# Attention and maxout feed-forward on one core: the start of batch 0 put in another order

## The chip, the cores and the metric

The kernel runs on one core of one Trainium2 chip. The metric is the device time of one execution in microseconds (us); the time given for a kernel is the median of its runs. A profiled execution also has a span, which runs from the first to the last recorded instruction and is a little shorter than the device time of that same execution.

## The reference

Two layers stand one behind the other. The first is attention with a softmax whose denominator has one more term; the second is a feed-forward layer that takes the maximum of three products.

```python
scores = scale * np.matmul(q, k.transpose(0, 1, 3, 2))
m = np.max(scores, axis=-1, keepdims=True)
e = np.exp(scores - m)
attn = e / (np.sum(e, axis=-1, keepdims=True) + np.exp(-m) + 1e-09)
return np.matmul(attn, v)
...
h = np.maximum(np.maximum(x @ w1, x @ w2), x @ w3)
return h @ w_out
```

q, k and v have 8 batches, 12 heads, 448 positions and 64 columns, in float32. x is the attention output with its heads side by side: 3584 rows of 768. The four weights are 768 x 768.

## The kernel before

**Tiling.** A batch's 12 heads are three groups of four heads, and a group is two pairs of heads. Groups are numbered through: 0, 1 and 2 are batch 0, group 3 is the first of batch 1, and there are 24. For one group the kernel loads k, q and v (POOL issues these DMAs, which turn float32 into float16 on the way), turns q and k over on TensorE (`transpose_pe`, L183, in two halves `pr` 0 and 1; `transpose_once`, L213, a whole q or k), and copies the result from PSUM to the tiles `KT` and `QT` (`evac`, L177, on ScalarE, "ACT", or VectorE, "DVE"). `scores` (L281) multiplies K by Q and takes the exponential on ACT into one of two buffers `e`. `av` (L523, by `av_tail` and `av_main`) multiplies the exponentials by V and then divides by the sum on DVE, for one pair of heads. `x_transpose_pe` (L387) turns the result over into `xT`, the input of the feed-forward. `prep_v` (L376) lays v out for `av` in three copies, `vx` and twice `vt`.

**Parts of batch 0.** While the data still come in, groups 0 to 2 are done in two parts of the query positions: the part "O" (192 columns) of each group and then the part "E" (256 columns). From group 3 on both parts go together ("EO").

**Feed-forward.** Its work lies in a list of pieces, and `fill` (L506) takes the next ones from it wherever the written order has a place for them. An `up_piece` (L430) is 12 matmuls of line 435 for one weight matrix and two blocks of columns, and its result goes into `hT` by a copy (first matrix) or a maximum (second and third) on DVE. For the part O of batch 0 there are nine of them: three with w1, then three with w2, then three with w3. Each weight matrix comes in three DMAs, and the last eight matmuls of a piece need the second and the third.

**Buffers.** `ps_s` has three PSUM buffers for scores and for `av`. `ps_b` has two, which the transposes, the turned results, the matmuls that only keep TensorE busy (`warm`, L163) and the feed-forward share in turn: a tile taken from it waits for the tile two places earlier to be read out.

**What sets the order.** The order on each engine is the order in which the code is written; nothing is rearranged. POOL issues all loads in one queue and does some copies in that same queue, so a load stands behind the copies written before it. Before the loop over parts (L537 to L592) POOL gets: the loads of groups 0 and 1, of v 0, of group 2, of v 1 and v 2 (L142 to L150), then the copies and loads of L529 to L535. The loop over `parts` runs for n = 0 to 5. Its steps for n = 0, 1 and 2 are written so that the second half of a group's transposes comes after that group's first scores, and the `av` of a group between the scores of the next one.

**Group 3.** The loop of L614 does a group in three visits: scores for some of the units, then (visits 0 and 1) `av` of the group before, then pieces of the feed-forward. In group 3 (`first`) a visit also turns over q and k of group 4.

```python
            if first and vi == 1:
                transpose_once(i + 1, "q", AC)
                fill(per)
                transpose_once(i + 1, "k", DV)
                per = 0
            elif i + 1 < PE_QK and vi < 2:
                transpose_once(i + 1, "qk"[vi], (AC, DV)[vi])
            fill(per)
```

These lines (L644 to L651) turn q of group 4 over in visit 0 by the second branch, and once more in visit 1 by the first branch, then k.

Of the kernel before, what the change touches and what calls it, by code (L numbers as in the profile page):

```python
# [21 lines left out]
def kernel(  # L22
# [20 lines left out]
    NG = H // GH  # L43
# [4 lines left out]
    NE, NO = 4 * HP, 3 * HP  # L48
# [7 lines left out]
    PE_QK = 7  # L56
# [44 lines left out]
    def load_qk(i, names="kq", prs=(0, NP)):  # L101
        b, g = groups[i]
        tiles = raw.setdefault(i, {})
        for nm in names:
            if nm not in tiles:
                t = ld_bufs[nm][i % NL]
                if nm == "q" and i < NF:
                    nc.vector.memset(t[:, 0 : NP * T + 2 : NP * T + 1, :], 0.0)
                tiles[nm] = t
            src = {"q": q, "k": k}[nm][b].rearrange("h s d -> (h s) d")  # L110
            src = src.rearrange("(g r x t) d -> g x r (t d)", g=NG, r=NP, x=P)[g]
            p0, p1 = prs
            nc.gpsimd.dma_start(  # L113
                out=tiles[nm][:, 1 : NP * T + 1].rearrange("x (r t) d -> x r (t d)", r=NP)[:, p0:p1],
                in_=src[:, p0:p1],
            )
# [16 lines left out]
    def load_weight(i, gs=(0, 1, 2)):  # L133
        w = (moe_w1, moe_w2, moe_w3, moe_w_out)[i]
        src = w.rearrange("(g hf p) f -> g p hf f", g=3, hf=2)
        for g in gs:
            nc.gpsimd.dma_start(out=w_sb[i][:, 2 * g : 2 * g + 2, :], in_=src[g])  # L137
# [5 lines left out]
    load_qk(0, "kq", (1, 2))  # L143
    ident16 = cpool.tile([128, 128], MMDT, name="ident16")
    make_identity(nc, ident16)
    load_qk(1)
    load_v(0)
    load_qk(2)
    load_v(1)
# [13 lines left out]
    def warm(n, cols=512):  # L163
        ps = ps_b.tile([128, 512], FP32, tag="b", name="warm")
        for _ in range(n):
            nc.tensor.matmul(
                out=ps[:, 0:cols], lhsT=wz[:, 0:128], rhs=wz[:, 0:cols], start=True, stop=True
            )
# [14 lines left out]
    def transpose_pe(i, pr, pool, k_eng, q_engs):  # L183


        def tile_of():
            if pool is ps_s:
                return ps_s.tile([128, 2, 1024], MMDT, tag="s", name="trT")[:, 0]
            return ps_b.tile([128, 1024], MMDT, tag="b", name="trT")

        kr, qr = raw[i]["k"], raw[i]["q"]
        kj = (0, 1, 2) if pr == 0 else (3, 4, 5, 6)
        qt = (-1, 1, 3, 5, 0, 2, 4, 6) if pr == 0 else (8, 10, 12, 7, 9, 11, 13)
        n = -(-len(qt) // len(q_engs))
        jobs = [(k_eng, "k", kj[0], kr, [2 * b for b in kj])]
        for e, eng in enumerate(q_engs):
            jobs.append((eng, "q", pr * 8 + e * n, qr, qt[e * n : (e + 1) * n]))
        if i not in KT:
            KT[i] = att_pool.tile([P, T * 128], MMDT, tag="KT", name="KT")
            QT[i] = att_pool.tile([P, (NB + 1) * 128], MMDT, tag="QT", name="QT")  # L200
        tps = [tile_of() for _ in jobs]
        for tp, (eng, nm, o, src, toks) in zip(tps, jobs):
            for j, t in enumerate(toks):
                nc.tensor.transpose(
                    out=tp[:, ts(j, 128)],
                    in_=src[:, t + 1 : t + 3, :].rearrange("x t d -> x (t d)"),
                    identity=ident16,
                )
        for tp, (eng, nm, o, src, toks) in zip(tps, jobs):
            dst = {"k": KT, "q": QT}[nm][i]  # L210
            evac(eng, dst[:, o * 128 : (o + len(toks)) * 128], tp[:, 0 : len(toks) * 128])
# [163 lines left out]
    def prep_v(i, eng):  # L375
        t = raw[i]["v"]  # L376
        vx, vt = v_buf[i % NV], vt_buf[i % NV]
        eng.tensor_copy(out=vx[:, :, :, 0:D], in_=t[:, :, 1:4, :])  # L378
        t2 = t.rearrange("p (r h) t d -> p r h t d", r=NP)
        eng.tensor_copy(out=vt[0:HP, :, 0:D], in_=t2[0:HP, :, 0, 4, :])  # L380
        eng.tensor_copy(out=vt[HP:P, :, 0:D], in_=t2[HP:P, :, 1, 0, :])
# [141 lines left out]
    def av(i, ej, pr, part):  # L523
        av_tail(i, ej, pr, PW[part])
        av_main(i, ej, pr, PW[part])

    warm(10)
    transpose_pe(0, 0, ps_s, DV, (AC, DV))
    prep_v(0, PL)  # L529
    load_weight(0, (0, 1))  # L530
    prep_v(1, PL)
    load_weight(0, (2,))
    load_qk(3)
    prep_v(2, PL)
    load_weight(1)  # L535

    parts = [(part, g) for part in "OE" for g in range(NG)]  # L537
    for n, (part, g) in enumerate(parts):
        ej = n % NEB
        pp, pg = parts[n - 1] if n > 0 else (None, None)  # L540
        scores(g, ej, (0, 1), part)
        if n < 3:
            if n == 0:
                warm(2)
            transpose_pe(g, 1, ps_b, DV, (DV,))
            scores(g, ej, (2, 3), part)
            if n > 0:
                av(pg, 1 - ej, 0, pp)
            if n == 1:
                transpose_pe(2, 0, ps_b, AC, (DV,))  # L550
            if n == 2:
                x_transpose_pe(0, "O")
            scores(g, ej, (4, 5), part)
            scores(g, ej, (6,), part)
            if n > 0:
                av(pg, 1 - ej, 1, pp)
            else:
                warm(4)
                transpose_pe(1, 0, ps_b, AC, (DV,))
                load_qk(4)  # L560
                load_weight(2)
                load_v(3)
        elif n == 3:
            av(pg, 1 - ej, 0, pp)
            x_transpose_pe(1, "O")
            av(pg, 1 - ej, 1, pp)
            scores(g, ej, (2, 3), part)
            x_transpose_pe(2, "O")
            add_up(0, NE, NO, [(i, f) for i in range(3) for f in (0, 2, 4)])
            fill(STEP)  # L570
            scores(g, ej, (4, 5), part)
            scores(g, ej, (6,), part)
            fill(STEP)
        else:
            scores(g, ej, (2, 3), part)
            av(pg, 1 - ej, 0, pp)
            if n == 4:
                transpose_once(3, "q", AC)
            else:
                x_transpose_pe(0, "E")  # L580
            fill(STEP)
            scores(g, ej, (4, 5), part)
            scores(g, ej, (6,), part)
            av(pg, 1 - ej, 1, pp)
            if n == 4:
                transpose_once(3, "k", AC)
            fill(STEP)
            if n == 4:
                shift_q(3, PL)
                load_v(4)  # L590
                load_qk(5)
                load_weight(3)  # L592


    visits = ((0, 1), (2, 3), (4, 5, 6))
# [18 lines left out]
    for i in range(3, NI):  # L614
        ej, pj = (i + 1) % NEB, i % NEB
        first = i == 3
        if PE_QK <= i + 2 < NI:
            transpose_dma(i + 2)
        if first:
            load_v(i + 2)  # L620
        for vi, units in enumerate(visits):
            n = 3 * i + vi
            scores(i, ej, units)
            if i == 4 and vi == 0:
                prep_v(i, DV)
            if vi < 2:
                av(i - 1, pj, vi, "E" if first else "EO")
            if vi == 1 and i > 3 * PE_X:
                x_transpose_dma(i - 1)
            if n in adds:  # L630
                add_batch(adds[n])
            per = STEP if first and vi < 2 else share(n)
            if vi == 0 and first:
                x_transpose_pe(1, "E")
            if vi == 2 and first:
                x_transpose_pe(i - 1, "E")
                fill(per / 2)
                prep_v(i, DV)
                add_up(0, 0, NE, [(w, f) for w in range(3) for f in (0, 2, 4)])
                add_out(0)  # L640
                per = share(n)
            if vi == 2 and 3 < i <= 3 * PE_X:
                x_transpose_all(i - 1)
            if first and vi == 1:  # L644
                transpose_once(i + 1, "q", AC)
                fill(per)
                transpose_once(i + 1, "k", DV)
                per = 0
            elif i + 1 < PE_QK and vi < 2:
                transpose_once(i + 1, "qk"[vi], (AC, DV)[vi])  # L650
            fill(per)  # L651
        if i + 1 < PE_QK:
            shift_q(i + 1, nc.gpsimd)
        if first:
            load_qk(i + 3)
        if i < 5:
            load_more(i + 3, i + 4)
        if 5 <= i + 1 < NI:
            prep_v(i + 1, nc.gpsimd)
        if PE_QK <= i + 2 < NI:  # L660
            shift_q(i + 2, nc.gpsimd)
        if i >= 5:
            load_more(i + 3, i + 4)
# [37 lines left out]
```

## Time and profile before

| What | Value |
|---|---|
| median of 4 runs | 344.26 us (343.77 to 346.33) |
| the profiled execution's own time | 344.13 us |
| its span | 342.2 us |
| TensorE (PE) busy | 329.9 us, 96% of the span |
| VectorE (DVE) busy | 187.2 us, 55% |
| ScalarE (ACT) busy | 151.9 us, 44% |
| GpSimd (POOL) busy | 148.9 us, 44% |
| granted TensorE clock | 1.0 of full speed |
| software DMA queue (POOL's loads) | 22.03 MB in float16, 29408 packets |

A row of the timeline gives the start and the length in us, the engine, the line of the code, the operation, what it writes and reads with shapes, how many instructions were merged, and in square brackets how long the engine stood idle before it and what ended that. A row of the chain gives start, length and what the end was waiting for at that time. A row of the windows gives a stretch, its length, and the busy time of an engine in it. "PEld" is TensorE's loading of weights, which runs beside its matmuls. Names are the code's: `trT` is a transposed q or k in PSUM, `stp` scores, `avp` the output of `av`, `xtp` a turned result, `p_i` a feed-forward piece, `ld_k`, `ld_q`, `ld_v` and `w` the loaded tiles.

### The profile page before, as it was taken

What the parts mean: (1) busy time and instruction counts of PE and PEld (TensorE: products, weight loads), DVE (VectorE), ACT (ScalarE), POOL (GpSimd) and SP (SyncE); (2) the same over time, 40 slices, a digit from 0 to 9 for tenths busy, and PEclk for the clock granted to TensorE, in tenths of its full rate; (3) what the DMA queues carried; (4) which work ended last, traced back from release to release, by engine and by line L of the source; (5) the groups of instructions that cost most, each with busy time, mean ns of one, the idle gap of its engine ahead of it and who ended that gap; (6) DMA issues with size and microseconds to landing.
All of it is one profiled execution on the core that took longest, in us unless ns stands there. A gap on an engine that the chain in (4) does not pass through costs nothing.

```text
span 342.2 us, 9832 instructions
## 1 busy us (share of the span) xinstructions
PE 329.9 (96%) x4183; PEld 199.5 (58%) x4183; DVE 187.2 (55%) x405; ACT 151.9 (44%) x181; POOL 148.9 (44%) x266
## 2 busy tenths in 40 slices
PE   6889999999999999999999999999999999999994
PEld 2668777866556555555555655555556655565552
DVE  2464566555556556556556456555556556465552
ACT  2668766764544444453544444543444444200000
POOL 8696578692771529264273377345154000000000
PEclk9999999999999999999999999999999999999999
DMA  7999999799999999979987999898974540133006
GB/s 97 176 196 208 202 206 185 94 171 193 159 117 108 164 217 157 159 103 208 147 117 83 211 201 150 131 113 202 135 109 41 124 125 4 33 74 96 0 19 166
DMA packets 84812, 46.19 MB, mean 135 GB/s; under 512 B 53280, under 2 KB 81312, under 8 KB 84768
## 3 DMA queue, kind: packets, MB, share of 16 engines
q0 software_dynamic: 29408, 22.03, 48.4%
q1 hardware_dynamic: 55120, 23.37, 37.4%
q8 instruction: 32, 0.52, 0.6%
q10 hardware_dynamic: 240, 0.16, 0.2%
q14 instruction: 12, 0.10, 0.1%
HBM read 44.04 MB, written 11.01 MB: 161 GB/s over the span
## 4 chain that ended last, share of the span: by engine, by line
PE 86%; DMA 6%; POOL 5%; issue 1%; ACT 1%; DVE 0%; POOLq 0%; ACTq 0%
PE p_i L435 46%; PE op_ps L459 16%; PE avp L352 11%; PE stp L295 10%; DMA w<-in_moe_w_dram 4%; DMA ld_v<-in_v_dram 2%; PE avp L335 2%; POOL ld_q L113 1%; POOL w L137 1%; POOL ld_k L113 1%; PE trT L220 1%; PE xtp L408 0%; POOL vx L378 0%; POOL ld_v L123 0%; ACT e L315 0%
## 5 line engine op out<-in xcount | busy, mean ns | idle before, releaser
L315 ACT ACTIVATE e<-stp 128x896 f16<-128x896 f32 (+4 forms) x171 | 144.5, 903 | 140.0 <-PE stp L295 139.8
L435 PE MATMUL p_i<-xT,w 128*128 128x448 f16 (+2 forms) x972 | 173.6, 332 | 1.3 <-DVE xT L401 0.6
L435 PEld LDWEIGHTS <-w 128*128 128x128 f16 x972 | 90.0, 98 | 69.1 <-issue 5.5
L240 POOL COPY QT<-QT 64x384 f16<-64x384 f16 (+1 forms) x84 | 46.7, 556 | 99.7 <-DMA QT<-ld_q 67.4
L446 DVE TENSOR_TENSOR hT<-hT,p_i 128x448 f16<-128x448 f16 (+2 forms) x96 | 59.6, 621 | 47.3 <-PE p_i L435 47.1
L459 PE MATMUL op_ps<-w,hT 128*128 128x384 f16 (+2 forms) x342 | 58.1, 323 | 0.0
L295 PE MATMUL stp<-QT,KT 64*64 64x448 f16 (+2 forms) x756 | 48.7, 338 | 2.0 <-DVE QT L181 1.8
L352 PE MATMUL avp<-vx,e 128*128 128x65 f16 x1152 | 45.4, 193 | 0.0
L459 PEld LDWEIGHTS <-hT 128*128 128x128 f16 x342 | 32.1, 98 | 22.7 <-issue 2.0
L466 DVE TENSOR_SCALAR o_sb<-op_ps 128x384 f32<-128x384 f32 (+2 forms) x57 | 31.2, 549 | 23.9 <-PE op_ps L459 23.7
L444 DVE CAST hT<-p_i 128x448 f16<-128x448 f32 (+2 forms) x48 | 30.0, 625 | 22.4 <-PE p_i L435 22.2
L352 PEld LDWEIGHTS <-e 128*128 128x128 f16 x1152 | 38.8, 97 | 2.3
L368 DVE TENSOR_TENSOR xn<-avp,rb 128x512 f16<-128x512 f32 (+1 forms) x54 | 34.1, 632 | 1.9
L295 PEld LDWEIGHTS <-KT 64*64 64x64 f16 x756 | 16.0, 105 | 26.7 <-issue 22.7
L362 DVE TENSOR_SCALAR rb<-avp 128x8 f32<-128x8 f32 (+1 forms) x54 | 8.9, 166 | 39.9 <-PE avp L352 39.8
L378 POOL COPY vx<-ld_v 128x768 f16<-128x768 f16 x22 | 18.0, 818 | 3.6 <-DMA ld_v<-in_v_dram 1.5
L335 PEld LDWEIGHTS <-e 64*64 64x64 f16 x768 | 14.7, 107 | 7.4 <-issue 0.6
L113 POOL DMA_DIRECT2D ld_q<-in_q_dram x25 | 18.1, 723 | 2.0 <-DMA w<-in_moe_w_dram 1.1
L113 POOL DMA_DIRECT2D ld_k<-in_k_dram x25 | 18.0, 720 | 1.9 <-POOLq L685 0.8
L126 POOL DMA_DIRECT2D ld_v<-in_v_dram x24 | 15.2, 634 | 2.1 <-DMA w<-in_moe_w_dram 1.3
L123 POOL DMA_DIRECT2D ld_v<-in_v_dram x24 | 15.1, 631 | 1.7 <-DMA w<-in_moe_w_dram 1.2
L335 PE MATMUL avp<-vt,e 64*64 64x65 f16 x768 | 15.6, 193 | 0.2 <-DVE xn L368 0.2
(41 smaller groups left out, 89.0 us busy)
## 6 DMA issues: line engine op xcount, KB each, us to landing
out_dram<-o_sb SPq DMA_DIRECT2D x54, 192.0 KB, 3.4
ld_v<-in_v_dram POOLq DMA_DIRECT2D x48, 128.0 KB, 4.6
ld_k<-in_k_dram POOLq DMA_DIRECT2D x23, 224.0 KB, 6.6
ld_q<-in_q_dram POOLq DMA_DIRECT2D x23, 224.0 KB, 7.5
w<-in_moe_w_dram POOLq DMA_DIRECT2D x9, 384.0 KB, 7.9
w<-in_moe_w_out_dram POOLq DMA_DIRECT2D x3, 384.0 KB, 8.8
xT<-xn SPq DMA_TRANSPOSE x18, 4.0
QT<-ld_q SPq DMA_TRANSPOSE x17, 6.0
```

Source lines behind the costliest of these rows:

```text
L113: nc.gpsimd.dma_start(out=tiles[nm][:, 1 : NP * T + 1].rearrange("x (r t) d -> x r (t d)", r=NP)[:, p0:p1], in_=src[:, p0:p1],)
L240: eng.tensor_copy(out=t[d0 : d0 + HP, o * 128 : (o + n) * 128], in_=t[s0 : s0 + HP, a * 128 : (a + n) * 128],)
L295: nc.tensor.matmul(out=stp[half * HP : half * HP + HP, par, j * qn : (j + 1) * qn], lhsT=k_block(i, pr, h2, x[half]), rhs=q_cols(i, pr, h2 ...
L315: nc.scalar.activation(out=dst, in_=src, func=AF.Exp, scale=scale)
L335: nc.tensor.matmul(out=ps[half * HP : half * HP + HP, hh, j * D1 : (j + 1) * D1], lhsT=eF[hh * HP : hh * HP + HP, o : o + HP], rhs=vt[hh * ...
L352: nc.tensor.matmul(out=ps[:, hh, j * D1 : (j + 1) * D1], lhsT=eF[:, o : o + 128], rhs=vx[:, 2 * pr + hh, (x[0]), 0:D1], start=False, stop= ...
L368: nc.vector.tensor_tensor(out=xn[i][:, pr, ws[0] : ws[0] + nw].rearrange("p j h d -> p h j d"), in0=acc[:, :, :, 0:D], in1=rb[:, :, 0:nw]. ...
L435: nc.tensor.matmul(out=p_i[:, j * qn : (j + 1) * qn], lhsT=w_sb[i][:, dc, ts(fc, 128)], rhs=xT[b][:, dc, q0 : q0 + qn], start=(dc == 0), s ...
L444: nc.vector.tensor_copy(out=dst, in_=src)
L446: nc.vector.tensor_tensor(out=dst, in0=dst, in1=src, op=ALU.max)
L459: nc.tensor.matmul(out=op_ps[:, 0:w], lhsT=hT[bp][:, fc, ts(t, 128)], rhs=wout_sb[:, fc, c : c + w], start=(fc == 0), stop=(fc == NFC - 1),)
L466: nc.vector.tensor_scalar(out=o_sb[:, c : c + w], in0=op_ps[:, 0:w], scalar1=1.0 / LAMBDA, scalar2=None, op0=ALU.mult,)
```

## The change

1. The load of group 1 is issued as four DMAs (k and q of pair 0, then of pair 1) and no longer as two.
2. In `transpose_pe` one block of q (token 6, which reaches into the second pair) goes from the first half to the second, so the first half turns 7 blocks of q and the second 8.
3. The copies of `prep_v(0)` go from POOL to DVE and to a later place, after the scores of group 1. On POOL `prep_v(2)` now comes ahead of `load_qk(3)`.
4. The part O of groups 0, 1 and 2 is written out. Both halves of group 0 are turned over before its first scores, all its scores follow, then 5 `warm` matmuls (before: 2 and 4 at two places). Both `av` of group 0 stand next to each other after the scores of group 1; those of group 1 lie around the scores of group 2, and the first `av` of group 2 comes ahead of the first scores of the part E. The second half of group 1's k is evacuated on ACT and no longer on DVE.
5. In group 3, q of group 4 is turned over once, in visit 0, and after the feed-forward piece of that visit instead of before it; k is turned over in visit 1 as before. The second transpose of q (7 transposes and one copy on ACT) is gone.

```diff
-    load_qk(1)
+    load_qk(1, "kq", (0, 1))
+    load_qk(1, "kq", (1, 2))
...
-        qt = (-1, 1, 3, 5, 0, 2, 4, 6) if pr == 0 else (8, 10, 12, 7, 9, 11, 13)
+        qt = (-1, 1, 3, 5, 0, 2, 4) if pr == 0 else (6, 8, 10, 12, 7, 9, 11, 13)
...
-            jobs.append((eng, "q", pr * 8 + e * n, qr, qt[e * n : (e + 1) * n]))
+            jobs.append((eng, "q", pr * 7 + e * n, qr, qt[e * n : (e + 1) * n]))
...
-    warm(10)
-    transpose_pe(0, 0, ps_s, DV, (AC, DV))
-    prep_v(0, PL)
     load_weight(0, (0, 1))
     prep_v(1, PL)
     load_weight(0, (2,))
+    prep_v(2, PL)
     load_qk(3)
-    prep_v(2, PL)
     load_weight(1)
...
+    S01, S23, S46 = ("s", (0, 1)), ("s", (2, 3)), ("s", (4, 5), (6,))
+    warm(10)
+    transpose_pe(0, 0, ps_s, DV, (AC, DV))
+    transpose_pe(0, 1, ps_b, DV, (DV,))
+    attend("O", 0, S01, S23, S46)
+    warm(5)
+    transpose_pe(1, 0, ps_b, AC, (DV,))
+    load_qk(4)
+    load_weight(2)
+    load_v(3)
+    attend("O", 1, S01)
+    transpose_pe(1, 1, ps_b, AC, (DV,))
+    attend("O", 1, S23, S46)
+    prep_v(0, DV)
+    attend("O", 1, ("v", 0, 0), ("v", 0, 1))
+    transpose_pe(2, 0, ps_b, AC, (DV,))
+    attend("O", 2, S01)
+    transpose_pe(2, 1, ps_b, DV, (DV,))
+    attend("O", 2, ("v", 1, 0), S23)
+    x_transpose_pe(0, "O")
+    attend("O", 2, S46, ("v", 1, 1), ("v", 2, 0))
+    attend("E", 0, S01)
+    x_transpose_pe(1, "O")
+    attend("E", 0, ("v", 2, 1), S23)
+    x_transpose_pe(2, "O")
...
-            if first and vi == 1:
-                transpose_once(i + 1, "q", AC)
+            if first:
                 fill(per)
-                transpose_once(i + 1, "k", DV)
                 per = 0
-            elif i + 1 < PE_QK and vi < 2:
+            if i + 1 < PE_QK and vi < 2:
                 transpose_once(i + 1, "qk"[vi], (AC, DV)[vi])
             fill(per)
```

`attend(part, g, ...)` calls `scores` for the units of an "s" step and `av` of part O for a "v" step (group, pair). From the last transpose of part O on, the order of the parts E is that of before, and so is everything after group 3.

More of the change, by code (lines that the diff above doesn't have):

```diff
@@ L532 @@
     load_weight(0, (2,))
+    prep_v(2, PL)
     load_qk(3)
-    prep_v(2, PL)
     load_weight(1)
[L537 to L540, printed above, removed]
-        scores(g, ej, (0, 1), part)
[L542 to L573, printed above, removed]
-        else:
[L575 to L592, printed above, removed]
@@ new lines, in attend @@
+    def attend(part, g, *steps):
+        ej = (g + (part == "E") * NG) % NEB
+        for st in steps:
+            if st[0] == "s":
+                for u in st[1:]:
+                    scores(g, ej, u, part)
+            else:
+                pg, pr = st[1:]
+                av(pg, pg % NEB, pr, "O")
+    S01, S23, S46 = ("s", (0, 1)), ("s", (2, 3)), ("s", (4, 5), (6,))
[3 more added lines that the diff above has]
+    attend("O", 0, S01, S23, S46)
@@ new lines @@
+    x_transpose_pe(1, "O")
+    attend("E", 0, ("v", 2, 1), S23)
+    x_transpose_pe(2, "O")
+    add_up(0, NE, NO, [(i, f) for i in range(3) for f in (0, 2, 4)])
+    fill(STEP)
+    attend("E", 0, S46)
+    fill(STEP)
+    for n in (4, 5):
+        ej, part, g, pp, pg = n % NEB, "E", n - 3, "E", n - 4
+        scores(g, ej, (0, 1), part)
+        scores(g, ej, (2, 3), part)
+        av(pg, 1 - ej, 0, pp)
+        if n == 4:
+            transpose_once(3, "q", AC)
+        else:
+            x_transpose_pe(0, "E")
+        fill(STEP)
+        scores(g, ej, (4, 5), part)
+        scores(g, ej, (6,), part)
+        av(pg, 1 - ej, 1, pp)
+        if n == 4:
+            transpose_once(3, "k", AC)
+        fill(STEP)
+        if n == 4:
+            shift_q(3, PL)
+            load_v(4)
+            load_qk(5)
+            load_weight(3)
```

## The prediction

> **What bounds the kernel now.** I first asked where TensorE (PE) stands still. The page's busy line by 40 slices, with the DMA line beside it:
>
> ```profile
> PE   6889999999999999999999999999999999999994
> ...
> DMA  7999999799999999979987999898974540133006
> ```
>
> PE is short of full only in the first slices and the last; DMA is full from the second slice on. The windows of the stretch after 46 us (stretch, its length, busy time of PE first) show it harder:
>
> ```profile
> 46.00:60.00 14.00, 14.00 (x229) 11.50 (x229) 9.37 (x22) 8.46 (x12) 10.75 (x19) 1.00 1.26 192
> 60.00:80.00 20.00, 20.00 (x361) 14.36 (x354) 11.58 (x25) 13.59 (x17) 15.92 (x29) 1.00 0.89 132
> 320.00:330.00 10.00, 10.00 (x55) 5.11 (x54) 5.60 (x9) 0.00 (x0) 0.00 (x0) 1.00 0.00 0
> ```
>
> All stretches between 46 and 336 us read like this, without idle time. What follows is fixed PE work, so the end moves by as much as PE's place at 46 us moves. The chain of waits says what sets that place:
>
> ```profile
> 26.32 13.97 DMA w<-in_moe_w_dram
> 40.29 0.05 issue
> 40.34 0.83 PE p_i L435 x8
> ...
> 43.21 0.93 ACT QT L179
> 44.14 0.04 issue
> 44.19 0.55 PE trT L220 x7
> ```
>
> The third DMA of w3, issued at 26.32, lands at 40.29 and frees the first piece with w3; behind it a copy on ACT holds PE once more. The timeline there:
>
> ```profile
> 38.47 0.55 PE L220 MATMUL trT<-ident,ld_q 128*128 128x128 f16 x7
> 39.66 0.49 PE L435 MATMUL p_i<-xT,w 128*128 128x192 f16 x4 [0.64 <-DVE xT L401]
> 40.34 0.83 PE L435 MATMUL p_i<-xT,w 128*128 128x192 f16 x8 [0.19 <-DMA w<-in_moe_w_dram]
> 42.06 0.55 PE L220 MATMUL trT<-ident,ld_q 128*128 128x128 f16 x7
> 42.45 1.15 PE L435 MATMUL p_i<-xT,w 128*128 128x192 f16 x12
> 43.21 0.93 ACT L179 ACTIVATE QT<-trT 128x896 f16<-128x896 f16 x1
> 44.19 0.55 PE L220 MATMUL trT<-ident,ld_k 128*128 128x128 f16 x7 [0.59 <-ACT QT L179]
> ```
>
> So 40.34 is a gate set by the loads. Time that PE wins before it is lost at it; time won behind it is kept. The same q is transposed at 38.47 and 42.06, and the second copy of it makes PE wait 0.59 us.
>
> **The change, part by part.** *Group 3, behind the gate (part 5).* The second q transpose goes: 7 instructions, 42.06 to 42.45 by the next start, -0.39 us. The wait of the k transpose goes, -0.59 us: its PSUM buffer was held by the second copy, queued behind two exponentials until 44.14. The remaining q transpose moves behind the gate with its piece: +0.39 us. Its copy (0.93 us) now stands ahead of visit 1's two exponentials: the transpose ends at about 41.75 (40.34 + 0.83 + 0.55), the copy at 42.68, the exponentials (1.73 us for two) at 43.55 and 44.41. The scores of visit 2, at about 44.15 by the new sum, need both their buffers; the second wants 44.41 where PE is there at about 44.35, so +0.10 us. The 0.64 us wait ahead of the piece also goes, because the piece takes the other `ps_b` buffer, but it lies before the gate and is worth nothing. Sum: -0.39 - 0.59 + 0.39 + 0.10 = **-0.49 us**. Bounds: -0.59 if the exponentials do not press, 0 if another wait of PE takes the place of the 0.59.
>
> *The loads, which set the gate (parts 1 and 3).* Up to w3 the same bytes go in nearly the same order through one queue: 6.6 MB in float16 (issue sizes: groups 0 to 4 459 kB each, v 0 to 2 262 kB each, three weights 1180 kB each). Two more issues cost POOL 4 x 0.57 - (0.71 + 0.72) = +0.85 us (0.56 and 0.57 us for a pair load, 0.71 and 0.72 us for a whole one), ahead of v 0. That is hidden while DMA has a backlog: by 8.1 us 1.41 MB were issued, while the stretches 2 to 8 us at 95, 131 and 143 GB/s moved 0.74 MB; without that cover it would cost the 0.85 us. In the rows POOL waits at an issue for the landing eight issues earlier (`ld_v` at 10.0 for group 1's `ld_k`, issued 4.13 and landing 5.6 us later). With two more issues ahead, every load behind them keeps its partner. Only v 1 and v 2 now wait for the quarters of group 1, whose landing still comes long before the stream reaches v.
>
> `prep_v(0)` leaves POOL, with its 0.66 us wait for v 0 (12.07 to 12.73), so w1 is issued at about 12, not 14.08. In exchange `prep_v(2)` (0.82 + 0.29 + 0.29, with gaps 1.4 us) stands ahead of group 3's load: 18.41 becomes 19.8. This is the thinnest place. By then 3.34 MB are issued, and the stretches up to 20.5 us have moved 3.0 MB, so the queue would be empty at about 22.2; a first packet came 1.3 us after its issue began (1.25 to 2.55), hence at 21.1. One microsecond is left: cost 0. From 21.2 us on the issues of w2, group 4 and w3 are as before (21.22). Gate: bound below -1.0 us (14 to 24 us ran at 190 GB/s, 26 to 30 us at 212: 10 us x 0.1), above +0.4 us (the four loads of group 1 at the pace of group 0's, 131 against 146 GB/s over 0.46 MB). I take 0, because the bytes, their order and the full DMA line stay.
>
> *The three copies of `prep_v(0)` on DVE.* By the DVE rows of line 378 to 381 they take 0.35 + 0.43 + 0.19 us, overlapping; between 14 and 15 us DVE has room. POOL's issues beside those rows (47.23 and 47.93) took 0.71 and 0.64 us, the usual length. The Trainium skill ("DMA: Bandwidth & Descriptors", section "SWDGE vs HWDGE vs iDMA") speaks against this edit: VectorE in its two-port mode locks GpSimd out of the memory into which it writes descriptors. By this rule an issue beside the copies would be up to 0.97 us longer, and the sum would still stand as long as the queue of loads is not empty.
>
> I take the rows: no cost on POOL, and on DVE at most 0.97 us, which would come out of the lateness that is free (below).
>
> *Batch 0 before the gate (parts 2 and 4).* Before, PE stood still 1.62 us at 7.09 for q of group 0's second pair, in all 1.9 us between 8 and 24, and 0.54 at 24.56. I walked the new order with these durations (12 transposes 0.66 us, first scores 0.30, an `av` 0.57, exponentials 0.81, q copies 0.62 to 0.69). Group 0's exponentials end at 11.3 (before 12.26), group 1's at 16.3 (before 17.9); then the q copy of group 2 stands behind six DVE operations for group 0's sums (two times 0.8 us), and group 2 starts at 17.95 (before 17.41). The last transpose of part O comes at 24.5; before, at 24.56. The walk may err by 1 us. Bounds: 2.6 us earlier if all idle time and one `warm` of 0.22 us went. That is worth 0 at the gate. And late, 1.7 us are free: PE came to w2's last DMA 0.32 us early (31.90 to 32.22) and would now be at the gate at about 38.9 (38.24, plus 0.2 for `xtp`, plus 0.49 for four matmuls), 1.4 us early. Beyond 1.7 each microsecond costs one.
>
> Total -0.49 us against the profiled 344.13 us (span 342.2, 1.93 around it), so 343.64. That run is 0.13 below the median of the four, 344.26; on the median I get **343.8 us**.
>
> **The rivals.** *A, the gate opens earlier.* If DMA really gains from w1 being queued two microseconds sooner, PE can follow by 1.4 us at most: 343.8 - 1.4 = 342.4. For it: rates of 131 to 163 GB/s up to 12 us against 210 later. Against: those low rates stand with full DMA slices and a growing backlog, so not for lack of issues. *B, slower: the queue runs dry at group 3's load.* The place is POOL behind `prep_v(1)` and `prep_v(2)`, which wait for v 1 and v 2 and have w1's third DMA and then everything else behind them. It decides from the point where group 3's load begins later than 20.9; v 1 landing at 16.36 had 0.88 us of waiting even before. If v 1 and v 2 land so late that DMA stands still 2.5 us, the gate moves by that: 343.8 + 2.5 = 346.3. Against: v 2's last byte is the 2.16th MB, which the rates shown have moved by 16.2; v 1 landed 1.5 us after its own place in that count, so v 2 comes at about 17.7, ahead of its copies. *C, the change does not do what it says:* the stall behind the gate is replaced, as by the ACT copy now in front of the exponentials. Then nothing is left: 344.2.
>
> **How the numbers follow.** Forecast 0.57, C 0.20, A 0.13, B 0.10. A measurement of this kernel tells about 0.5% (1.72 us) from no change, so the forecast and C are "same", 0.77; A is faster, 0.13; B slower, 0.10. The predicted time is the forecast's, 343.8. The forecast's own range is 343.4 to 344.2; the range takes in C, A's 342.4, and the gate's +0.4 and part of B above: 342.3 to 345.0.
>
> **What would show it.** Right: one group of 7 q transposes near 41.2 and none at 42; no idle time ahead of the k transpose; the eight matmuls of the first w3 piece still released by DMA, near 40.3, after a PE wait of over a microsecond; PE full from then on. Wrong: those matmuls released well before 39.5 (A) or after 41 (B, with low GB/s near 20 to 23 us); or no DMA wait there at all, which would mean that PE is more than 1.7 us late and my walk of batch 0 fails.

## The result, and the profile after

| | before | changed |
|---|---|---|
| median of all runs | 344.64 us (64 runs) | 343.57 us (43 runs) |
| lowest run | 343.11 us | 342.19 us |
| ratio | | 0.9963, 95% interval 0.995 to 0.9976 |
| profiled execution, span | 344.13, 342.2 us | 343.85, 342.1 us |

By the ratio the change saves 0.37%, 1.3 us, with an interval of 0.8 to 1.7 us; by the medians it is 1.07 us. The whole interval lies on the side of a saving, but the saving is under the 0.5% that the prediction took as the least it could tell. The forecast was 343.8 us, in a range of 342.3 to 345.0. Two executions among the experiments were disturbed and stand in no ratio: 841 us, the profiled one with 15 warm matmuls, whose profile is not read, and 661 us, one with all but part 5.

The busy lines by 40 slices of the changed kernel look as before:

```profile
PE   8788899999999999999999999999999999999994
...
DMA  7999999799899999969989999998970550124006
```

The windows behind 46 us (stretch, its length, busy time of PE first) again have no idle time:

```profile
46.00:60.00 14.00, 14.00 (x221) 11.54 (x222) 9.25 (x22) 8.60 (x11) 10.73 (x19) 1.00 1.26 196
60.00:336.00 276.00, 276.00 (x3285) 158.53 (x3274) 154.39 (x307) 114.54 (x134) 104.51 (x188) 1.00 0.81 125
```

The chain of waits has the same gate, later than before:

```profile
26.16 14.99 DMA w<-in_moe_w_dram
41.19 0.83 PE p_i L436 x8
42.03 0.39 PE trT L221 x7
```

The timeline there, with the transposes, the pieces and the turned results (`xtp`) of visit 2:

```profile
39.40 0.49 PE L436 MATMUL p_i<-xT,w 128*128 128x192 f16 x4
41.19 0.83 PE L436 MATMUL p_i<-xT,w 128*128 128x192 f16 x8 [1.30 <-DMA w<-in_moe_w_dram]
41.87 0.55 PE L221 MATMUL trT<-ident,ld_q 128*128 128x128 f16 x7
43.31 1.15 PE L436 MATMUL p_i<-xT,w 128*128 128x192 f16 x12
44.29 0.55 PE L221 MATMUL trT<-ident,ld_k 128*128 128x128 f16 x7
45.47 0.40 PE L396 MATMUL xtp<-ident,xn 128*128 128x128 f16 x4
```

and the same turned results in the kernel before:

```profile
45.36 0.40 PE L395 MATMUL xtp<-ident,xn 128*128 128x128 f16 x4
```

There is one group of q transposes, the wait ahead of the k transpose is gone, and PE waits 1.30 us for w3. From the gate to `xtp` it was 45.36 - 40.34 = 5.02 us and is now 45.47 - 41.19 = 4.28 us: 0.74 us less. But the gate opened 0.85 us later in this execution, so the two spans are alike (342.2 and 342.1). Two things move at once, and the experiments part them.

### The profile page after: what moved, and what is told of

Its sections match the earlier page's. It is cut to its first block, busy times and chain, and to the rows that moved or that the text cites. A ratio compares the mean times of both kernels' runs of the same rounds, so it can differ in the third digit from the quotient of the medians.

```text
span 342.1 us, 9827 instructions
## 1 busy us (share of the span) xinstructions
PE 329.8 (96%) x4175; PEld 199.6 (58%) x4175; DVE 187.1 (55%) x407; ACT 151.4 (44%) x181; POOL 148.4 (43%) x265
## 4 chain that ended last, share of the span: by engine, by line
PE 87%; DMA 6%; POOL 5%; issue 1%; DVE 0%; POOLq 0%
PE p_i L436 46%; PE op_ps L460 16%; PE avp L353 11%; PE stp L296 10%; DMA w<-in_moe_w_dram 4%; DMA ld_v<-in_v_dram 2%; PE avp L336 2%; POOL ld_q L113 1%; POOL ld_k L113 1%; POOL w L137 1%; PE trT L221 1%; PE xtp L409 0%; POOL vx L379 0%; POOL ld_v L123 0%; POOL ld_v L126 0%
## 5 line engine op out<-in xcount | busy, mean ns | idle before, releaser
L296 PE MATMUL stp<-QT,KT 64*64 64x448 f16 (+2 forms) x756 | 47.6, 338 | 2.4 <-DVE QT L182 2.0
L379 POOL COPY vx<-ld_v 128x768 f16<-128x768 f16 x21 | 17.2, 818 | 8.5 <-issue 4.2
```

The costliest lines, as they stand in the source:

```text
L296: nc.tensor.matmul(out=stp[half * HP : half * HP + HP, par, j * qn : (j + 1) * qn], lhsT=k_block(i, pr, h2, x[half]), rhs=q_cols(i, pr, h2 ...
```

## The experiments

**Part 5 in two forms.** First the kernel before with nothing but part 5.

```diff
-            if first and vi == 1:
-                transpose_once(i + 1, "q", AC)
+            if first:
                 fill(per)
-                transpose_once(i + 1, "k", DV)
                 per = 0
-            elif i + 1 < PE_QK and vi < 2:
+            if i + 1 < PE_QK and vi < 2:
```

> The kernel before with part 5 alone (q of group 4 turned over once, behind its piece). Theory (the last DMA of w3 is a gate; only what lies behind it or moves the gate counts): from the gate (first of the eight matmuls) to the turned results of visit 2, 5.02 us becomes 4.28 us, so 0.74 us less than before, 0.2%, with the gate itself unchanged on average. Rival (part 5 is everything the change gives): the whole 0.37% of the changed kernel, 1.3 us. Rival (the ACT copy in front of the exponentials takes it back): no change, and a wait of PE on ACT at the scores of visit 2.

Measured: 343.69 us (before 344.71), ratio 0.9958 (0.9929 to 0.9988). In its profile the gate opens at 39.92 and `xtp` starts at 44.20, 4.28 us later as expected, and no wait on ACT stands at the scores. The time, 1.4 us less with an interval of 0.4 to 2.4, does not tell the theory's 0.74 from the first rival's 1.3; it lies nearer the rival. Then the least edit, the second q transpose alone taken out:

```diff
             if first and vi == 1:
-                transpose_once(i + 1, "q", AC)
                 fill(per)
```

> The kernel before without the second transpose of q of group 4, all else as before: the one q transpose stays in front of the gate, so PE still comes to the gate at 40.15 at the earliest. Theory: behind the gate 0.39 us of transposes and 0.76 us of waiting go (from the start of the second piece with w3 to the transpose of k 1.74 us becomes 0.98), so 1.15 us less than before, 0.33%, in every execution, whether the gate is early or late. Rival (what helps is that PE comes sooner to the gate): clearly less than the 0.42% of part 5 alone.

Measured: 342.96 us (before 344.80), ratio 0.9951 (0.9924 to 0.9979); the rival's smaller gain did not come. Its timeline:

```profile
40.34 0.83 PE L435 MATMUL p_i<-xT,w 128*128 128x192 f16 x8 [0.20 <-DMA w<-in_moe_w_dram]
42.06 1.15 PE L435 MATMUL p_i<-xT,w 128*128 128x192 f16 x12
43.05 0.55 PE L220 MATMUL trT<-ident,ld_k 128*128 128x128 f16 x7
44.23 0.40 PE L395 MATMUL xtp<-ident,xn 128*128 128x128 f16 x4
```

The gate opened at 40.34 as in the profile of before, and PE's rows from 31 us to there agree to 0.03 us, so this is the cleanest pair: 45.36 becomes 44.23, and the span 342.2 becomes 341.1. The gain of 1.1 us is the transposes (0.39) and the time from the second piece's start to the k transpose (1.74 becomes 0.99).

**Everything but part 5.** The changed kernel with the five lines of group 3 as before.

```diff
-            if first:
+            if first and vi == 1:
+                transpose_once(i + 1, "q", AC)
                 fill(per)
+                transpose_once(i + 1, "k", DV)
                 per = 0
-            if i + 1 < PE_QK and vi < 2:
+            elif i + 1 < PE_QK and vi < 2:
```

> The changed kernel without part 5: loads, copies and the order of batch 0 as changed, q of group 4 turned over twice as before. The transposes in visit 0 stand ahead of the gate again and the wait on the ACT copy is back. Theory: slower than the changed kernel by 0.74 us. Against the kernel before: no change if the gate stays where it was (0.0 us), 0.5 us faster if the earlier issue of w1 opens the gate earlier on average, 0.85 us slower if the gate is as late as in the changed kernel's one profile (41.19 against 40.34).

Measured: 344.26 us (before 344.71), ratio 0.9992 (0.9967 to 1.0017). Gate at 41.10, `xtp` at 46.12: 5.02 us, as before. Against the changed kernel it is 1.0 us more, known to about 1.0, where 0.74 was expected. Loads and the order of batch 0, four of the five parts, bring nothing that the times show; part 5 alone gives what the whole change gives.

**Is the time in front of the gate free?** Ten, then five more warm matmuls ahead of group 1.

```diff
-    warm(5)
+    warm(15)
```

> The changed kernel with 15 instead of 5 warm matmuls ahead of group 1: ten more of 0.216 us, 2.2 us of PE work in front of the gate. Theory: PE waited 1.10 us for w2 at 33.2 and 1.30 us for w3 at 41.2, together 2.4 us, so the 2.2 us are swallowed: no change (within 0.3 us), and the two DMA waits shrink by 2.2 us together. Rival (the order and the pace of batch 0 count): 2.2 us slower, 0.6%.

```diff
-    warm(5)
+    warm(10)
```

> The changed kernel with 10 instead of 5 warm matmuls ahead of group 1, 1.08 us more of PE work in front of the gate. With the gate between 39.9 and 41.2, and PE at about 38.8 if it waited for nothing, 1.1 to 2.4 us are free. Theory: no change, within 0.3 us, and the waits at w2 and w3 shrink by 1.08 us together. Rival (batch 0's pace counts one to one): 1.1 us slower.

Measured: with 15, 344.61 us (before 344.71), ratio 1.0003 (0.9983 to 1.0023); with 10, 344.26 us (before 344.80), ratio 0.9986 (0.9964 to 1.0009). Against the changed kernel's median of 343.57 that is about 1.0 us for 2.16 us of matmuls and 0.7 us for 1.08: less was swallowed than expected. The waits of PE for weights (in total, times, longest), first of the changed kernel and then of that with 10:

```profile
PE p_i L436 <- DMA w<-in_moe_w_dram: 2.4, 2, 1.3
```
```profile
PE p_i L436 <- DMA w<-in_moe_w_dram: 1.8, 2, 1.5
```

The waits shrank by 0.6 us, not 1.08. In this one profile the wait for w2 is gone, and PE starts the first piece with w3 at 39.02, where it was 39.40 without the five extra matmuls; both remaining waits are at that piece, whose gate opened at 41.50 and not 41.19, and `xtp` is later by these 0.31 us alone:

```profile
39.63 0.34 PE L436 MATMUL p_i<-xT,w 128*128 128x192 f16 x2 [0.29 <-DMA w<-in_moe_w_dram]
41.50 0.83 PE L436 MATMUL p_i<-xT,w 128*128 128x192 f16 x8 [1.53 <-DMA w<-in_moe_w_dram]
...
45.78 0.40 PE L396 MATMUL xtp<-ident,xn 128*128 128x128 f16 x4
```

So this execution swallowed the matmuls. The times say otherwise: by the ratios (0.9963 and 1.0003) the dose of 2.16 us cost 1.4 us, and both intervals together leave 0.6 to 2.2. The prediction had 1.7 us free in front of the gate, so 2.16 should have cost at most 0.5. PE time in front of the gate is not free, contrary to what I had expected; that it counts less than one to one is likely, but not shown by the times, and the dose of 1.08 us (0.8 us by the ratios, known to about 0.9) shows nothing by itself.

**Is it the queue that sets the gate?** w3 ahead of k and q of group 4.

```diff
-    load_qk(4)
     load_weight(2)
+    load_qk(4)
```

> The changed kernel with the three DMAs of w3 issued ahead of k and q of group 4 (459 kB in float16, 2.2 us at 205 GB/s). Theory (the gate is set by the bytes ahead of it in the queue): the gate's DMA lands about 2.2 us earlier, near 39.0; PE arrives at 39.9 without a wait and gains up to 1.3 us, less what q of group 4 is then late for its transpose (landing near 41.2 where PE would want it at 40.7): 0.8 us less than the changed kernel, and a DMA wait at the transpose of q. Rival (the gate is not what holds the end): no change.

Measured: 342.91 us (before 344.71), ratio 0.9929 (0.9899 to 0.9959). The timeline (PEld is the weight loading of the same transposes):

```profile
38.91 1.15 PE L436 MATMUL p_i<-xT,w 128*128 128x192 f16 x12
...
40.68 0.39 PEld L221 LDWEIGHTS <-ld_q 128*128 128x128 f16 x7 [0.85 <-DMA ld_q<-in_q_dram]
40.69 0.56 PE L221 MATMUL trT<-ident,ld_q 128*128 128x128 f16 x7 [0.62 <-DVE hT L447]
```

The first piece with w3 runs through in one row of 12, without a wait: the gate is gone, and q of group 4, now behind w3, is the next to be late (the PE row names a DVE operation that ended at about the same time and reads another buffer; the weight loading beside it names the load). Both as expected. Against the changed kernel's 0.9963 the gain is 1.2 us, known to about 1.1. Then with only q ahead of w3:

```diff
-    load_qk(4)
+    load_qk(4, "q")
     load_weight(2)
+    load_qk(4, "k")
```

> The changed kernel with the loads of group 4 parted: q, then the three DMAs of w3, then k. w3 has 229 kB less ahead of it than in the changed kernel (1.1 us at 205 GB/s), and q of group 4 comes ahead of it again. Theory (the gate is set by the bytes ahead of it, and PE could be there 1.3 us sooner): no wait for q at its transpose, a wait at the gate of 0 to 0.5 us, 1.1 us less than the changed kernel and 0.3 to 0.6 us less than the kernel with w3 ahead of both; about 0.7% less than the kernel before. Rival (PE's way through batch 0 is the bound once w3 moves): the same as with w3 ahead of both.

Measured: 342.22 us (before 344.80), ratio 0.9929 (0.9912 to 0.9947). No wait for w3 or q is left at the gate; `xtp` starts at 43.97, and PE waits 1.11 us for w2 at 32.91, where the kernel with w3 ahead of both waited 1.07. Against the changed kernel it is 1.2 us less, as expected and clear of the intervals (0.4 to 1.9). The 0.3 to 0.6 us over the kernel with w3 ahead of both did not show in the ratios, which are equal; in the profiles `xtp` is 0.33 us earlier. So the times leave the rival standing.

**The order on POOL.** POOL's rows of the kernel before:

```profile
18.41 0.71 POOL L113 DMA_DIRECT2D ld_k<-in_k_dram  x1
19.10 0.72 POOL L113 DMA_DIRECT2D ld_q<-in_q_dram  x1
19.87 0.82 POOL L378 COPY vx<-ld_v 128x768 f16<-128x768 f16 x1
```

and of the changed kernel:

```profile
18.42 0.82 POOL L379 COPY vx<-ld_v 128x768 f16<-128x768 f16 x1
19.19 0.29 POOL L381 COPY vt<-ld_v 64x128 f16<-64x128 f16 x1
19.54 0.29 POOL L382 COPY vt<-ld_v 64x128 f16<-64x128 f16 x1
19.77 0.71 POOL L113 DMA_DIRECT2D ld_k<-in_k_dram  x1
```

Group 3's load starts 1.4 us later. The windows (last column GB/s), first before, then changed:

```profile
22.00:24.00 2.00, 2.00 (x58) 1.46 (x50) 1.76 (x8) 1.06 (x2) 2.00 (x3) 1.00 1.21 188
24.00:26.00 2.00, 1.46 (x16) 1.06 (x14) 0.82 (x3) 0.99 (x1) 2.00 (x4) 1.00 1.20 203
26.00:28.00 2.00, 2.00 (x42) 1.60 (x41) 0.86 (x2) 1.49 (x2) 0.86 (x2) 1.00 1.16 209
```
```profile
22.00:24.00 2.00, 2.00 (x52) 1.40 (x51) 1.68 (x7) 1.06 (x2) 2.00 (x4) 1.00 1.15 175
24.00:26.00 2.00, 1.51 (x23) 1.14 (x16) 0.96 (x3) 1.02 (x1) 2.00 (x4) 1.00 1.00 157
26.00:28.00 2.00, 2.00 (x40) 1.49 (x40) 0.70 (x2) 1.34 (x2) 0.82 (x2) 1.00 1.13 177
```

Three kernels test it: the old loads and POOL copies under the new order, the one line of `prep_v(2)` put back, and the changed kernel again beside it.

```diff
-    load_qk(1, "kq", (0, 1))
-    load_qk(1, "kq", (1, 2))
+    load_qk(1)
...
+    prep_v(0, PL)
     load_weight(0, (0, 1))
     prep_v(1, PL)
     load_weight(0, (2,))
+    load_qk(3)
     prep_v(2, PL)
-    load_qk(3)
     load_weight(1)
...
-    prep_v(0, DV)
```

> The changed kernel with the loads and POOL's copies of before: group 1 whole, prep_v(0) on POOL ahead of w1, prep_v(2) behind the load of group 3; the order of batch 0 and part 5 stay. Theory (bytes and their order set the landings): same as the changed kernel within 0.3 us. Rival (the later issue of group 3 in the changed kernel lets the queue run thin near 22 to 26 us, 157 GB/s there against 203): 0.5 to 0.9 us faster than the changed kernel. Rival (w1 issued two microseconds sooner opens the gate earlier): 0.5 us slower.

Measured: 343.70 us (before 344.80), ratio 0.9966 (0.9948 to 0.9985); 192 GB/s from 24 to 26 us, gate at 40.05. By the time this is the theory (the changed kernel has 0.9963); by the profile it is the first rival's fuller stretch.

```diff
-    prep_v(2, PL)
     load_qk(3)
+    prep_v(2, PL)
```

> The changed kernel with one line moved back: the load of group 3 ahead of prep_v(2) on POOL. Theory (the queue of loads runs thin where group 3's load waits behind those copies): 190 to 205 GB/s between 24 and 26 us, w3 landing about 1 us earlier (gate near 40.1 instead of 41.2), and the time 0.5 to 1.0 us below the changed kernel. Rival (the dip has another cause, or PE cannot use an earlier gate): same as the changed kernel.

> The changed kernel as it is, beside the next three. Expected: 0.9963 of the kernel before again; in its profile 150 to 170 GB/s between 24 and 26 us, and w3 landing about 1 us later than in the kernels that issue group 3's load ahead of prep_v(2).

Measured: with the line put back 343.04 us (before 344.85), ratio 0.9945 (0.9924 to 0.9966); the changed kernel 343.44 us, 0.9948 (0.9925 to 0.997). The window with the line put back:

```profile
24.00:26.00 2.00, 1.51 (x23) 1.13 (x16) 0.96 (x3) 1.02 (x1) 1.47 (x4) 1.00 1.18 207
```

and its gate opens at 39.42. Over all thirteen profiles the split is without exception. With group 3's load behind the copies (six profiles) the stretch from 24 to 26 us moved 130 to 168 GB/s; with it ahead (seven) 192 to 207. From 22 to 28 us it was 1.02 to 1.10 MB against 1.15 to 1.25; the changed kernel's 1.02 and the 1.20 of before differ by 0.18 MB, 0.9 us at 205 GB/s, which is about the 0.85 us by which its gate was later. In the kernels that keep w3 behind k and q of group 4, the gate opened at 41.19, 41.10, 41.50 and 40.61 with the late load, at 40.34, 40.34, 39.92, 40.05 and 39.42 with the early one: 1.1 us apart on average. So the loss of rate is shown in the profiles. In the times it is not: the two kernels that differ in this line alone are 0.4 us apart by medians, and their ratios 0.0003 apart, each known to 0.002. The profiled executions lean to the two sides: with the late load five of six took longer than the median of their kernel (0.5 us on average), with the early one five of seven took less (0.4 us on average). So 1.1 us may well be too much for an ordinary execution.

One line in the profile of the second look at the changed kernel says that the gate is not all. Its span is 343.1 us though its `xtp` starts at 44.89. From the waits of PE and of DVE after 46 us:

```profile
DVE o_sb L467 <- DMA out_dram<-o_sb: 3.6, 1, 3.6
...
PE p_i L436 <- DVE o_sb L467: 1.4, 1, 1.4
```

At 199 us a store of results held DVE for 3.6 us and, through it, PE for 1.4. DVE waited for a store in eight of the thirteen profiles, up to 2.2 us in the others; PE stood still for it in this one alone.

**Both load orders.** The line put back, and q, w3, k:

> As the last, and w3 issued between q and k of group 4. Theory: w2 lands near 32.1, where PE waits for it at most 0.3 us, and w3 near 39, where PE arrives at 38.9, so that no more than 0.5 us of waiting is left at both together: about 342.2 less 0.8, that is 341.4 us, 1% below the kernel before. Rival (another wait takes the place): 342.2, as with the load of group 3 late.

Measured: 341.85 us (before 344.85), ratio 0.992 (0.9891 to 0.9949), the fastest of all. Its timeline:

```profile
31.49 1.24 PE L436 MATMUL p_i<-xT,w 128*128 128x192 f16 x12
...
38.15 0.49 PE L436 MATMUL p_i<-xT,w 128*128 128x192 f16 x4
38.94 0.83 PE L436 MATMUL p_i<-xT,w 128*128 128x192 f16 x8 [0.30 <-DMA w<-in_moe_w_dram]
```

0.30 us of waiting for w3 is left, and no wait at w2. Against the changed kernel the gain is 1.5 us (0.4 to 2.6 by the two intervals). Then the kernel before with part 5 and q, w3, k alone:

> The kernel before with two small edits alone: part 5 (q of group 4 once, behind its piece), and w3 issued between q and k of group 4; batch 0 and its loads as before. Theory (the way through batch 0 is hidden in front of the loads): as good as the kernel with the new batch 0 and both load orders, 341.4 us, within 0.4 us. Rival (the new order of batch 0 brings something once the gate is gone): 0.5 to 1 us slower than that kernel.

Measured: 342.51 us (before 344.85), ratio 0.9928 (0.9901 to 0.9955); `xtp` at 43.80, 0.58 us behind that of the last kernel, because PE waited 0.78 us for w2 at 32.74. The medians are 0.66 us apart, the rival's figure and not the theory's 0.4, but the intervals overlap; whether the new order of batch 0 helps once the gate is gone stays open. The kernel differs from the last one in its loads too, not in batch 0 alone.

**Place and end.** The start of `xtp` and the span in each profile:

| kernel | gate opens | `xtp` starts | span | span less `xtp` |
|---|---|---|---|---|
| before | 40.34 | 45.36 | 342.2 | 296.8 |
| changed | 41.19 | 45.47 | 342.1 | 296.6 |
| second q transpose out | 40.34 | 44.23 | 341.1 | 296.9 |
| part 5 alone | 39.92 | 44.20 | 341.3 | 297.1 |
| all but part 5 | 41.10 | 46.12 | 342.7 | 296.6 |
| old loads | 40.05 | 44.33 | 341.0 | 296.7 |
| group 3's load put back | 39.42 | 43.69 | 340.4 | 296.7 |
| w3, then q and k | no wait | 44.30 | 341.0 | 296.7 |
| q, w3, k | no wait | 43.97 | 340.9 | 296.9 |
| both load orders | 38.94 | 43.22 | 340.0 | 296.8 |
| before with two edits | no wait | 43.80 | 340.7 | 296.9 |
| 10 warm matmuls | 41.50 | 45.78 | 342.4 | 296.6 |
| changed, second look | 40.61 | 44.89 | 343.1 | 298.2 |

Twelve of thirteen ends follow PE's place at 45 us to half a microsecond; the thirteenth has the 1.4 us at 199 us.

## Why the prediction was right, and where its sizes were off

*Right: what bounds the kernel.* PE without idle time from 46 us on, and the end moving with its place there: the last column of the table. *Right: the gate is w3's third DMA.* It was so in all nine profiles that keep w3 behind k and q of group 4, and moving w3 in the queue moved or removed it.

*Right in mechanism, too small: the sum behind the gate.* -0.49 us was foreseen, -0.74 measured. The stall was taken as the 0.59 us of idle time in the row, but the matmuls' ends are modelled; from start to start the piece and the stall together fell from 1.74 to 0.98 us, that is 0.76. And the 0.10 us for the ACT copy in front of the exponentials did not come: the scores of visit 2 show no wait. The copy began 1.27 us behind the gate where the sum had 1.41, and the two exponentials ended 3.80 us behind it where the sum had 4.07, because it put the durations end to end while the rows overlap:

```profile
42.46 0.92 ACT L180 ACTIVATE QT<-trT 128x896 f16<-128x896 f16 x1 [2.01 <-PE trT L221]
43.27 1.72 ACT L316 ACTIVATE e<-stp 128x896 f16<-128x896 f32 x2
```

*Wrong: the gate term.* I took 0, with +0.4 at most from slower pair loads. The gate opened 0.85 us later in the profile, at 41.19, behind the 41 that the prediction had named as a sign of rival B. It was B's place and not B's path: group 3's load began at 19.77 us, as foreseen and not later than B's 20.9, and v 2 was not late. "One microsecond is left: cost 0" failed although its count held: by the windows 3.33 MB had moved by 22 us, and by then group 3's load and the first of w2 had been issued behind the 3.34 MB that the prediction counted. The rate fell all the same from 22 us on. So a count of bytes does not give the rate; what does is not shown here. In time this came far from B's 2.5 us, and the medians do not show it.

*Not put to the test: the copies on DVE.* In the changed profile they ran from 13.62 to 14.28 us, and POOL issued no load between 13.0 and 17.68, so the run shows nothing on an issue beside them.

*Right: batch 0.* The walk gave group 0's exponentials ending at 11.3, group 1's at 16.3, group 2's first scores at 17.95 and the last transposes at 24.5; the changed profile has 10.83, 15.95, 17.86 and 24.72. It is no earlier at its end than before, and without part 5 the change gives 0.9992. What did not hold is that 1.7 us of lateness are free: by that the 15 warm matmuls should have cost 0.5 us at most, and they cost 0.6 to 2.2.

*Not settled: the rest.* The ratio says 1.3 us (0.8 to 1.7), the segment behind the gate 0.74, and the profiles have a later gate on top. One reason that the profiles allow is that before, PE came to the gate at 40.15 and could not have used an earlier opening, while with part 5 it comes at 38.6 to 40.0 and can (in the profile of part 5 alone it was there at 38.69 and passed at 39.92). How often the gate opens that early in unprofiled runs was not measured, so this stays argued.

*Luck in the number.* 343.8 us was reached from a median of four runs, 344.26, while 64 runs gave 344.64; and the gain was taken as 0.49 us where about 1.1 to 1.3 was measured. The two errors have opposite effects, and the distance of 0.2 us from the measured 343.57 owes much to that.

## What to carry to other kernels

When one engine runs without idle time from some point to the end, find the last wait in front of that point: work taken away behind it counts in full, and work reordered in front of it brought nothing here that the times show. But idle time in front of it, read from one profile, is not free to use: 2.16 us of work put there cost 0.6 to 2.2. The one edit that counted took out work done twice, and removing it alone gave the whole gain; the larger rewrite around it gave none that could be measured. A queue of loads that by a count of bytes is never empty can still lose rate at one place: look at its rate in stretches of two microseconds before a load is put behind other work of the engine that issues it.

## What the runs showed of the hardware

The loads lost rate while by count the queue was not empty: 175 GB/s between 22 and 24 us and 157 between 24 and 26 in the changed kernel, against 205 and 207 with one line put back, and 130 in the kernel with q, w3, k. There the issues of w2 began at 21.11 us and yet the stretch from 24 to 26 stayed short; why loads already issued did not fill it is open. And a store of results can hold PE: 3.6 us of waiting on DVE, 1.4 us on PE, at 199 us of one execution.
